# Attention beside Strassen-Winograd products: two visits of eight key tiles for every head, and QKV sums kept in DRAM

## The chip, the cores and the metric

One core of one Trainium2 chip runs the kernel in a single launch. The time is device microseconds of one execution. TensorE (PE) does the matrix products and loads its weights beside them (PEld), VectorE (DVE), ScalarE (ACT) and GpSimd (POOL) do the elementwise work, and SyncE (SP) issues the DMA transfers. PSUM holds the products' results in eight banks of 128 x 512 float32 values.

## What is computed

```python
def _A_ref(x, wqkv, wo):             # x 1 x 2048 x 1024, wqkv 1024 x 3072, wo 1024 x 1024
    H = 32; Dh = 32
    qkv = (x @ wqkv).reshape(B, S, 3, H, Dh).transpose(2, 0, 3, 1, 4)
    q, k, v = qkv[0], qkv[1], qkv[2]
    p = softmax(einsum("bhqd,bhkd->bhqk", q, k) * Dh ** -0.5)
    o = einsum("bhqk,bhkd->bhqd", p, v)
    return o.transpose(0, 2, 1, 3).reshape(B, S, D) @ wo
def _B_ref(x, dft_seq_re, dft_seq_im, dft_hid_re, dft_hid_im):
    a = einsum("bsd,ed->bse", x, dft_hid_re)
    b = einsum("bsd,ed->bse", x, dft_hid_im)
    return einsum("ts,bse->bte", dft_seq_re, a) - einsum("ts,bse->bte", dft_seq_im, b)
out = concatenate([_A_ref(...), _B_ref(...)], axis=-1)
```

## The kernel before

There are two kinds of work for TensorE. The dense parts are QKV (`qkv`), the product over the hidden dimension (`dense1`), the product over the sequence (`dense2`) and the output projection (`project`). Each is one level of a Winograd form with seven products instead of eight, numbered p = 1 to 7. Each float32 operand is split into a high and a low part of a faster format (`halves`: a cast and a subtraction), and three matmuls (high-high, low-high, high-low) make one product. A group of 12 or 24 such matmuls fills one PSUM bank, which is then evicted. The list `fills` holds these matmuls in their order; 6720 of them run.

The other kind is attention over 32 heads, in three streams. S (`scores`) makes the scores of a block of queries with 1024 keys in two matmuls (line 1322); VectorE takes the row maxima (line 1328) and ScalarE the exponentials and their sums (line 1331). T (`transposed`) makes the transposed scores, 16 key tiles of 128 keys by four query blocks of 512 (line 1447), and ScalarE turns each of these 64 products into a tile of exponentials (line 1456). V, the visits, multiplies the exponentials of some key tiles with V in column strips of 32 (line 1479) into one bank, and VectorE adds the bank to the head's output (lines 1499 and 1501). A visit starts only when the exponentials of its tiles are there, save the last one.

Rings limit what runs ahead. The exponentials have 23 tiles in heads 0 to 7 (5 `ptl`, 18 `pt`), and a head has visits of 5, 5 and 6 key tiles (`ENDS`). From head 8 on (`H2`) eight more tiles (`ptm`, pool `pt2`) come from memory that the QKV stage held as slots 12 to 15, and a head has two visits of eight (`ENDS2`). S and T have two PSUM buffers each, and the banks `pd` of fills and visits two.

QKV runs in twelve steps (`STEPS`). Steps 0 to 4 take the first three pairs of Q/K blocks (`PAIRS`) and V before attention starts. Steps 5 to 9 take the other five pairs in the order p = 1, 2, 6, 5, 3, and steps 10 and 11 take p = 7 and p = 4 for all pairs and V. A late pair's running sum X lies in a slot of SBUF (16 to 19, and 15 + b - `PAIRS` in general). For p = 7 two kept sums are loaded from DRAM through a ring of four `c` tiles (`CR`, function `kept`), and for the Q/K groups the third of them stays in its `c` tile until p = 4 of the same group, which follows at once: the groups of p = 7 and p = 4 alternate. In `dense1`, sums of rows 0 to 3 lie in slots 16 to 19 and those of rows 4 to 7 go by DRAM (`Far`, arrays `x_d`).

The order of all instructions is written out when the kernel is built, by a planner (`Plan`) that imitates the engines with fixed costs. For TensorE it picks among the heads of the streams and the next fill: a visit first, then T, then S, and a fill if none of these can start, or if the fills lag behind `nf / (FILL - RES) <= done / ATT`. Some constants steer it: `LEAD` and `SST` hold S back when it is too far ahead of T, `STOCK` (us) and `PATIENCE` put a visit off until enough work is queued on ScalarE, and `MARGIN` adds time to the landing of a DMA before VectorE's work on it is placed. The other engines, and SyncE's queue of DMAs, get the order that the imitated run gave; each engine then runs its list in order.

Of the kernel before, what the change touches and what calls it, by code (L numbers as in the profile page):

```python
# [16 lines left out]
P = 128  # L17
S = 2048
D = 1024
H = 32  # L20
# [4 lines left out]
NPT, NPT2 = 23, 8  # L25
H2 = 8
# [4 lines left out]
NLOW = 5  # L31
ENDS, ENDS2 = (0, 5, 10, 16), (0, 8, 16)
# [193 lines left out]
def kernel(  # L226
# [32 lines left out]
    u_d = [[dram.tile([P, NB], F32, name=f"u_d{g}_{k}") for k in (2, 3, 4)] for g in range(24)]  # L259
# [3 lines left out]
    x_d = [[{w: dram.tile([P, NB], F32, name=f"x_d{i}_{m}_{w}") for w in (1, 6, 5)} for m in range(2)] for i in range(4)]  # L263
# [8 lines left out]
    def slot(i, shape, dt=F32R):  # L272
        if i < 12:
            return big.tile(shape, dt, name=f"slot{i}", tag=f"slot{i}")
        if i < 16 and "pt2" in late:
            return op_pool().tile(shape, dt, name=f"slot{i}", tag=f"slot{i}")
        if i < 20:
            att()
            return late["sums" if i > 15 else "low"].tile(shape, dt, name=f"slot{i}", tag=f"slot{i}")
# [70 lines left out]
    def more():  # L350

        if "pt2" not in late:
            late["low"].release()
            late["pt2"] = tc.alloc_tile_pool(name="pt2", bufs=1, reuse_waits="tile")
        return late["pt2"]

# [7 lines left out]
    SUMS = (16, 17, 18, 19)  # L364
# [13 lines left out]
    SST = 12  # L378
    LEAD = 4
    PATIENCE = 2  # L380
    STOCK = 2.4
# [4 lines left out]
    ATT = H * (128 * MM + 16 * PV) + (3 * H2 + 2 * (H - H2)) * SWITCH  # L386
# [64 lines left out]
    slots = [[] for _ in range(40)]  # L451
# [169 lines left out]
    def qkv():  # L621
        VR, SG = Ring(NV), Ring(2)
        sq, tx, t1x = ([[] for _ in range(8)] for _ in range(3))
        sv, u_st = [[] for _ in range(4)], [[[], [], []] for _ in range(24)]
# [28 lines left out]
        def load_x(x, k):  # L653
            where[0] = ahead if x < 5 else within
            p = STEPS[x][0]
            if x < 5:
                i = 8 * ((x + 1) % 2) + k
                i = i if i < 12 else 20 + i
            else:
                i = (8 * (x - 5) + k) % 12 if x < 11 else (16, 8)[k // 4] + k  # L660
            XS[x, k] = moving(i, x_terms(p, k, x >= 5), (tx_d[k], tx[k]) if x == 3 else (t1x_d[k], t1x[k]) if x == 2 else None)

        def load_v_weight(x, c):
            where[0] = ahead if x < 5 else within
            p = STEPS[x][0]
            WV[x, c] = moving((28 if x in (1, 3) else 12 if x == 10 else 0 if x == 11 else 36) + c, w_terms(p, lambda i, j: wv[i, 4 * j + c], sv_d[c], sv[c]), (sv_d[c], sv[c]) if p == 6 else None)
# [83 lines left out]
        def gather(p, g, result, early, scale=None):  # L750
# [3 lines left out]
            whole_u3 = g < 16  # L754
# [11 lines left out]

            if p == 7:
                U4, U2 = kept(2), kept(0)
            elif p == 4:
                U3 = u3.pop(g) if whole_u3 else kept(1)  # L770

            def finish(ps, last):
                if p == 5 and early:
                    box = {}
                    old, users = ER.take()

                    def product(e="DVE"):
# [12 lines left out]
                    att_gate.extend([c, e, u_st[g][0][-1]])  # L790
                    return e
                if p == 1:
# [45 lines left out]
        def qk_group(x, W, b, n):  # L838
# [52 lines left out]
        for x, (p, blocks, v) in enumerate(STEPS[:10]):  # L891
# [35 lines left out]
            if x == 4:  # L927
                for u in ahead[0].users + slots[28:]:
# [6 lines left out]
        for x in (10, 11):  # L935
            for t in range(8):
                v_group(x, t)
                if x == 11 and t < 4:
                    load_x(11, 4 + t)
                elif x == 10 and t < 2:  # L940
                    for k in range(2):
                        load_x(10, 4 + 2 * t + k)
                elif x == 10 and 2 <= t < 6:
                    load_x(11, t - 2)
                    load_v_weight(11, t - 2)
# [115 lines left out]
    def dense1():  # L1061
# [26 lines left out]
        def load_b(x, n):  # L1088
            p = ORDER[x]
            B[x][n] = moving((8 * x + n) % 12, b_terms(p, n), (t1_d[n], t1[n]) if p == 6 else None)  # L1090
# [5 lines left out]
        for x, p in enumerate(ORDER):  # L1096
            for i in range(8):
# [4 lines left out]
                if p == 1:  # L1102
                    X[i] = accs(SUMS[i]) if i < 4 else [Far(x_d[i - 4][m]) for m in range(2)]
# [13 lines left out]
    def load_ab(step, k):  # L1117
# [11 lines left out]
        AB[step, k] = moving((8 * (7 + step) + k) % 12, terms, (t2_d[m][k], t2[m][k]) if p == 6 else None)  # L1129
# [47 lines left out]
    def op_pool():  # L1177
        if "op" not in late:
            att().release()
            qk0.release()  # L1180
            late["pt2"].release()
# [5 lines left out]
    def behind():  # L1187

        over.extend(o for h in o_st for o in h)
        for i in (*range(12, 16), *range(20, 28)):  # L1190
# [6 lines left out]
    def project():  # L1197
# [60 lines left out]
        for x, p in enumerate(ORDER):  # L1258
            for i in range(8):
                j, t = divmod(i, 4)  # L1260
                if p == 1 and i % 2 == 0:
                    X[i // 2] = accs(16 + i // 2)
                if p == 7 and i % 2 == 0:
                    Y[i // 2] = accs(12 + i // 2)
# [33 lines left out]
    def scores(h):  # L1298
# [12 lines left out]
        for n, (qt, c) in enumerate([(k % 4, k // 4) for k in range(8)] + [divmod(k, 2) for k in range(8, 32)]):  # L1311
# [30 lines left out]
            if n == 5 and h:  # L1342
                sums(h - 1)
# [87 lines left out]

    def transposed(h):
        moved = mine[h][4]
        todo, ends_with = [], []
        po = {}
        oold, ouse = ot_r.take()
        ends = ENDS if h < H2 else ENDS2
        for t in range(NS):
            for j in range(4):
# [9 lines left out]
                def ex(box=box, here=here):  # L1449
                    if here < NLOW:  # L1450
                        box["t"] = att_low().tile([P, NB], F32, name="ptl", bufs=NLOW)
                    elif here < NPT:
                        box["t"] = att().tile([P, NB], F32, name="pt", bufs=NPT - NLOW)
                    else:
                        box["t"] = more().tile([P, NB], F32, name="ptm", bufs=NPT2)
# [3 lines left out]
                def more_exp(a=a, ex=ex, here=here, users=users, box=box, t=t, j=j):  # L1459
# [3 lines left out]
                    return t, j, box, e, pt_r.users[here], a  # L1463
# [3 lines left out]
                if t + 1 in ends and j >= 4 - PEND:  # L1467
# [3 lines left out]
            if t + 1 in ends:  # L1471
                load, vuse = vts[h]
                t0 = ends[ends.index(t + 1) - 1]

                def pv(k, part, t=t, t0=t0):
                    if k == t0:
                        po["p"] = psD.tile([P, NB], F32, name="pd")
                    for _, j, box, *_ in part:
                        nc.tensor.matmul(  # L1479
                            po["p"][j * DH : j * DH + DH, :], VT[h][:, k, :], box["t"], start=(k == t0), stop=(k == t),  # L1480
                            tile_position=(0, j * DH),
                        )

                visit = []
                for k in range(t0, t + 1):
                    if k == t:
                        todo += [m() for m, _ in ends_with]
                    part = [x for x in todo if x[0] == k]
                    visit.append(op("PE", PV + (SWITCH if k == t0 else 0), lambda k=k, part=part, pv=pv: pv(k, part),
                                    [*load[: t // 4 + 1], *(x[3] for x in (todo if k == t0 else part)), *(x[1] for x in (ends_with if k == t0 else ()))],  # L1490
                                    [vuse, *(x[4] for x in part)]))
                ends_with = []
                v = visit[-1]
                todo = []

                def gather_o(t0=t0):
                    if t0 == 0:
                        po["o"] = att_low().tile([P, NB], F32, name="ot", bufs=2)
                        nc.vector.tensor_copy(po["o"], po["p"])
                    else:  # L1500
                        nc.vector.tensor_tensor(out=po["o"], in0=po["o"], in1=po["p"], op=ALU.add)

                e = op("DVE", EVAC, gather_o, [v] + (oold if t0 == 0 else []), [ouse], -1)
                streams["V"].append((visit[0], h, e, visit[1:]))
            if t % 4 == 3 and h + 2 < H:
                load_qk_op(h + 2, 1, t // 4, [Tops[h][-1], Sops[h][-1]])
        if h + 2 < H:
# [3 lines left out]
            load_v(h + 2)  # L1511
        return e, po, ouse
# [19 lines left out]
    for h in range(H):  # L1532
        if h == H2:
            pt_r.n %= NPT
            pt_r.users.extend(sum((slots[i] for i in range(12, 16)), []) for _ in range(NPT2))
        if h + 1 < H:
            scores(h + 1)
        else:
            sums(h)
        result(h, *transposed(h))  # L1540
# [15 lines left out]
    while nf < len(fills) or any(place[n] < len(s) for n, s in streams.items()):  # L1556
# [19 lines left out]
        pl.MARGIN["DVE"] = 3 if heads and t_on[0] else 2  # L1576
# [52 lines left out]
        if ok:  # L1629
# [5 lines left out]
            if n == "V":  # L1635
                banks.append(heads[n][2])
# [43 lines left out]
```

## Time and profile before

| what | value |
|---|---|
| median of 3 runs | 2942.34 us (2941.63 to 2942.66) |
| the profiled execution | 2942.34 us, span of its instructions 2940.6 us |
| granted TensorE clock | 1.000 |
| matmuls on TensorE | 14922 |
| DMA | 585 MB on SyncE's queue, share 61.8% |

In the rows of the profile, a group reads: line, engine, operation, output<-input by the program's names, count, then busy time in us, the mean of one in ns, and the idle time just before them with what ended it. `psS` and `psT` are the banks of the streams S and T, `pd` that of fills and visits, `qs`, `ks` and `qx` are Q and K, `c` a loaded sum, `e` an evicted result. A window's row gives for each engine the busy time and the number of instructions in the stretch.

### The profile page before, as it was taken

The numbers are of one execution on the slowest core, as the hardware profiler recorded it, in microseconds if no ns is written. First come the engines' busy times: TensorE is split into PE (matmuls) and PEld (weight loads), VectorE is DVE, ScalarE is ACT, GpSimd is POOL, SyncE is SP. The second block draws the span as 40 slices with busy tenths as digits, with TensorE's granted clock in tenths as the row PEclk, the third lists the DMA queues.
The fourth block names the chain that finished last, engine by engine and source line by source line (L and its number), as shares of the span: only waits on it lengthen the run. The fifth ranks groups of instructions, "written<-read, shape, count | busy, mean of one in ns | idle before, by whom it ended". The sixth has DMA issues, their size and how long they took to land.

```text
span 2940.6 us, 45778 instructions
## 1 busy us (share of the span) xinstructions
PE 2931.5 (100%) x14922; PEld 2151.9 (73%) x14922; DVE 2275.1 (77%) x3103; ACT 2271.7 (77%) x4322; POOL 956.6 (33%) x746
## 2 busy tenths in 40 slices
PE   9999999999999999999999999999999999999999
PEld 7887777677777777777777777777777777677787
DVE  6778888788877877877677888787787788886685
ACT  5348888888888888888888888888888888886331
POOL 2323435222204432231112454433112454454142
PEclk9999999999999999999999999999999999999999
DMA  9975658666637655675434776655434786665753
GB/s 348 356 249 183 200 183 276 227 213 225 218 103 229 217 176 164 212 226 166 158 101 147 239 231 205 189 180 169 129 113 132 216 270 200 194 182 191 264 194 126
DMA packets 393880, 587.96 MB, mean 200 GB/s; under 512 B 112782, under 2 KB 114574, under 8 KB 393518
## 3 DMA queue, kind: packets, MB, share of 16 engines
q1 hardware_dynamic: 393644, 585.05, 61.8%
q8 instruction: 120, 1.97, 0.3%
q14 instruction: 116, 0.95, 0.1%
HBM read 421.30 MB, written 163.59 MB: 199 GB/s over the span
## 4 chain that ended last, share of the span: by engine, by line
PE 98%; DVE 1%; DMA 1%; ACT 0%; SPq 0%; issue 0%; DVEq 0%; ACTq 0%
PE pd L421 44%; PE psT L1447 16%; PE psS L1322 16%; PE pd L1479 15%; PE psT L421 6%; DVE negm L1328 0%; DMA er<-in_xa 0%; DVE l L531 0%; DMA qs<-qk_d 0%; PE psT L443 0%; ACT psS L1331 0%; DVE h L528 0%; PE pd L443 0%; ACT slot L527 0%; DVE slot L531 0%
## 5 line engine op out<-in xcount | busy, mean ns | idle before, releaser
L1328 DVE TENSOR_REDUCE negm<-psS 128x1 f32<-128x1024 f32 x1024 | 1242.8, 1221 | 226.4 <-PE psS L1322 215.2
L1331 ACT ACTIVATE psS<-psS,negm 128x1024 f32<-128x1024 f32 x1024 | 1223.9, 1195 | 71.8 <-DVE negm L1328 70.0
L421 PE MATMUL pd<-slot,h 128*128 128x512 f32 x3360 | 1144.0, 390 | 0.0
L1456 ACT ACTIVATE pt<-psT 128x512 f32<-128x512 f32 x1296 | 782.6, 697 | 260.1 <-PE psT L1447 237.2
L1447 PE MATMUL psT<-qs,ks 128*128 128x512 f32 x2048 | 794.3, 394 | 1.3 <-DMA qs<-qk_d 1.3
L421 PEld LDWEIGHTS pd<-slot,h 128*128 128x128 f32 x3360 | 630.7, 188 | 132.0
L421 PE MATMUL pd<-slot,l 128*128 128x512 f32 x1680 | 654.6, 390 | 0.0
L507 POOL TENSOR_TENSOR raw<-raw,g 128x512 f32<-128x512 f32 x295 | 382.6, 1304 | 483.8 <-DVE l L531 63.8
L1447 PEld LDWEIGHTS psT<-qs,ks 128*128 128x128 f32 x2048 | 381.8, 188 | 137.3 <-issue 45.3
L1322 PE MATMUL psS<-ks,qs 128*128 128x512 f32 x1552 | 473.4, 390 | 1.2 <-ACT psS L1331 1.2
L531 POOL TENSOR_TENSOR l<-raw,h 128x512 fp32r<-128x512 f32 x157 | 202.5, 1290 | 554.6 <-PE psT L1447 236.6
L531 POOL TENSOR_TENSOR slot<-raw,slot 128x512 fp32r<-128x512 f32 x156 | 201.0, 1293 | 518.0 <-DVE slot L528 146.3
L421 PEld LDWEIGHTS pd<-slot,l 128*128 128x128 f32 x1680 | 315.3, 188 | 67.0 <-issue 0.8
L1479 PE MATMUL pd<-pt,vt 128*32 128x512 f32 x2592 | 345.8, 594 | 0.0
L1322 PEld LDWEIGHTS psS<-ks,qs 128*128 128x128 f32 x1552 | 290.8, 188 | 64.0 <-ACT psS L1331 3.8
L1331 ACT ACTIVATION_READ_ACCUMULATOR psS<-psS,negm 128x1 f32 x1024 | 321.6, 314 | 0.0
L1456 ACT ACTIVATE ptm<-psT 128x512 f32<-128x512 f32 x392 | 242.6, 715 | 49.7 <-PE psT L1447 46.7
L1456 ACT ACTIVATE ptl<-psT 128x512 f32<-128x512 f32 x360 | 223.5, 708 | 31.0 <-PE psT L1447 30.2
L1479 PEld LDWEIGHTS pd<-pt,vt 128*32 128x32 f32 x2592 | 89.4, 110 | 180.3 <-issue 168.2
L421 PE MATMUL pd<-slot,slot 128*128 128x512 f32 x768 | 193.0, 391 | 0.0
L421 PEld LDWEIGHTS pd<-slot,slot 128*128 128x128 f32 x768 | 144.1, 188 | 31.2
L528 DVE CAST h<-raw 128x512 fp32r<-128x512 f32 x321 | 149.1, 467 | 14.5 <-PE pd L421 12.3
(139 smaller groups left out, 2323.8 us busy)
## 6 DMA issues: line engine op xcount, KB each, us to landing
raw<-in_ct SPq DMA_DIRECT2D x224, 256.0 KB
g<-in_ct SPq DMA_DIRECT2D x128, 256.0 KB
c<-u_d SPq DMA_DIRECT2D x120, 256.0 KB
qk_d<-e SPq DMA_DIRECT2D x52, 512.0 KB
qs<-qk_d SPq DMA_DIRECT2D x128, 192.0 KB
ks<-qk_d SPq DMA_DIRECT2D x128, 192.0 KB
raw<-ab_d SPq DMA_DIRECT2D x96, 256.0 KB
g<-ab_d SPq DMA_DIRECT2D x80, 256.0 KB
```

The source lines that it names most:

```text
L421: nc.tensor.matmul(box["ps"], a[1]((a[0].hi, a[0].lo)[u]()), b[1]((b[0].hi, b[0].lo)[v]()), start=k == 0, stop=k == n - 1)
L507: return (nc.gpsimd if e == "POOL" else nc.vector).tensor_tensor(out=dest(), in0=dest() if a is None else a.get(), in1=other["q"] if "q" i ...
L528: return nc.vector.tensor_copy(hi(), raw())
L531: return (nc.gpsimd if e == "POOL" else nc.vector).tensor_tensor(out=lo(), in0=raw(), in1=f(hi()), op=ALU.subtract)
L1322: nc.tensor.matmul(p[:, i * NB : i * NB + NB], (QX[0] if own else QS[h % 2])[:, qt * P : qt * P + P], KS[h % 2][:, c * 1024 + i * NB : c * ...
L1328: nc.vector.tensor_reduce(out=ST["negm"][:, c, qt : qt + 1], in_=box["p"], axis=AX.X, op=ALU.max, negate=True)
L1331: nc.scalar.activation(box["p"], box["p"], AF.Exp, bias=ST["negm"][:, c, qt : qt + 1], accum_out=ST["sums"][:, c, qt : qt + 1])
L1447: nc.tensor.matmul(box["p"], KS[h % 2][:, t * P : t * P + P], QS[h % 2][:, j * NB : j * NB + NB], start=True, stop=True)
L1456: nc.scalar.activation(box["t"], box["p"], AF.Exp)
L1479: nc.tensor.matmul(po["p"][j * DH : j * DH + DH, :], VT[h][:, k, :], box["t"], start=(k == t0), stop=(k == t), tile_position=(0, j * DH),)
```

## The change

Every head gets visits of eight key tiles: `H2` is 0, and a list `CUTS` of cumulated key tiles over all heads takes the place of `ENDS`. The ring of exponentials has 31 tiles from the first head on, 13 of them in the pool `atl`; the pool `pt2` is gone. To free the memory, slots 16 to 19 are given up in the QKV stage and in `dense1`: the sums of the late pairs are stored in DRAM after p = 1, 6 and 5 and loaded again for p = 2, 6, 5 and 3, and `dense1` treats rows 0 to 3 as it did rows 4 to 7. The third sum of a Q/K group is stored at p = 7 and loaded at p = 4. All groups of p = 7 now come before those of p = 4, first V then Q/K at p = 7, first Q/K then V at p = 4, with the x pieces of p = 4 loaded among the Q/K groups of p = 7. Slots are renumbered. The small work of a head's sums (`sums`) is created in `transposed` rather than in `scores`. The planner's constants `SST`, `LEAD`, `STOCK` and `MARGIN` change.

```diff
-NPT, NPT2 = 23, 8
-H2 = 8
+NPT, NPT2 = 31, 8
+H2 = 0
-NLOW = 5
-ENDS, ENDS2 = (0, 5, 10, 16), (0, 8, 16)
+NLOW = 13
+BLOCKS, BLOCKS2 = (8, 8), (8,)
+CUTS = []
+for k in range(H2):
+    CUTS += [16 * k + sum(BLOCKS[: i + 1]) for i in range(len(BLOCKS))]
+while not CUTS or CUTS[-1] < 16 * H:
+    CUTS.append(min(16 * H, (CUTS[-1] if CUTS else 0) + BLOCKS2[len(CUTS) % len(BLOCKS2)]))
...
-    SUMS = (16, 17, 18, 19)
+    SUMS = (12, 13, 14, 15)
...
-    SST = 12
-    LEAD = 4
+    SST = 14
+    LEAD = 1
     PATIENCE = 2
-    STOCK = 2.4
+    STOCK = 1.4
...
-    ATT = H * (128 * MM + 16 * PV) + (3 * H2 + 2 * (H - H2)) * SWITCH
+    ATT = H * (128 * MM + 16 * PV) + len(CUTS) * SWITCH
...
-                i = (8 * (x - 5) + k) % 12 if x < 11 else (16, 8)[k // 4] + k
+                i = (8 * (x - 5) + k) % 12 if x < 11 else (12, -4)[k // 4] + k
...
-            whole_u3 = g < 16
+            whole_u3 = False
...
+            stored = p in (2, 3, 5, 6) and A is None
             if p == 7:
                 U4, U2 = kept(2), kept(0)
+            elif stored:
+                U = kept({2: 3, 6: 3, 5: 0, 3: 2}[p])
...
+                if A is None and p in (1, 5, 6):
+                    box = {}
+                    old, users = ER.take()
+                    i = {1: 3, 6: 0, 5: 2}[p]
+                    def keep():
+                        box["y"] = pre.tile([P, NB], F32, name="e", tag="e", bufs=NE)
+                        if p > 1:
+                            combine(box["y"], U[0](), ps(), ALU.add, scale)
+                        elif scale is None:
+                            nc.vector.tensor_copy(box["y"], ps())
...
+                    e = evac_op(keep, last, ER, [users, *(U[1] if p > 1 else [])], [*old, *([U[2]] if p > 1 else [])])
+                    u_st[g][i].append(op("SP", ISSUE, lambda: nc.sync.dma_start(u_d[g][i], box["y"]), [e], [users], rank, 256))
+                    return e
+                if stored:
+                    return result(ps, last, U[0], U[1], [U[2]], ALU.add)
...
-                    X[2 * b], X[2 * b + 1] = accs(15 + b - PAIRS)
+                    X[2 * b] = X[2 * b + 1] = None
...
-        for x in (10, 11):
-            for t in range(8):
+        for x, p in ((10, 7), (11, 4)):
+            for t in range(8 if x == 10 else 0):
                 v_group(x, t)
...
-        for b in range(8):
-            W = [piece(w_terms(p, lambda i, j: wqk[b + 8 * i][:, 4 * j : 4 * j + 4, :], None, None)) for p in (7, 4)]
-            for n in range(2):
-                qk_group(10, W[0], b, n)
-                qk_group(11, W[1], b, n)
+            for b in range(8):
+                W = piece(w_terms(p, lambda i, j: wqk[b + 8 * i][:, 4 * j : 4 * j + 4, :], None, None))
+                for n in range(2):
+                    qk_group(x, W, b, n)
+                if x == 10:
+                    load_x(11, (b + 4) % 8)
+            if x == 10:
+                for c in range(4):
+                    load_v_weight(11, c)
+        for t in range(8):
+            v_group(11, (t + 4) % 8)
...
-                    X[i] = accs(SUMS[i]) if i < 4 else [Far(x_d[i - 4][m]) for m in range(2)]
+                    X[i] = accs(SUMS[i]) if i < 0 else [Far(x_d[i][m]) for m in range(2)]
...
-                if t + 1 in ends and j >= 4 - PEND:
+                if 16 * h + t + 1 in CUTS and j >= 4 - PEND:
                     ends_with.append((more_exp, a))
...
-        pl.MARGIN["DVE"] = 3 if heads and t_on[0] else 2
+        pl.MARGIN["DVE"] = 2.5 if heads and t_on[0] else 1
```

More of the change, by code (lines that the diff above doesn't have):

```diff
@@ L274, in slot @@
             return big.tile(shape, dt, name=f"slot{i}", tag=f"slot{i}")
-        if i < 16 and "pt2" in late:
+        if i < 16:
+            att()
+            return late["low"].tile(shape, dt, name=f"slot{i}", tag=f"slot{i}")
+        if i >= 40:
             return op_pool().tile(shape, dt, name=f"slot{i}", tag=f"slot{i}")
-        if i < 20:
-            att()
-            return late["sums" if i > 15 else "low"].tile(shape, dt, name=f"slot{i}", tag=f"slot{i}")
         if i < 28:
@@ L1430, in load_v @@
         vts[h] = (made, users)
+    PO = {}
+    todo, ends_with = [], []
     def transposed(h):
         moved = mine[h][4]
[L1434 removed]
         po = {}
[L1436 to L1437 removed]
+        PO[h] = (po, *ot_r.take())
+        if not todo:
+            sums(h)
         for t in range(NS):
@@ L1470, in transposed @@
                     todo.append(more_exp())
[L1471 to L1504, printed above, removed]
@@ L1532 @@
     for h in range(H):
-        if h == H2:
-            pt_r.n %= NPT
-            pt_r.users.extend(sum((slots[i] for i in range(12, 16)), []) for _ in range(NPT2))
         if h + 1 < H:
             scores(h + 1)
-        else:
-            sums(h)
-        result(h, *transposed(h))
+        transposed(h)
     dense1()
```

97 lines of the change are left out of this document (65 added, 32 removed).

## The prediction

> **What bounds the kernel now.** I read the page first: engines, slices, the chain of work that ended last.
>
> ```profile
> span 2940.6 us, 45778 instructions
> PE 2931.5 (100%) x14922; PEld 2151.9 (73%) x14922; DVE 2275.1 (77%) x3103; ACT 2271.7 (77%) x4322; POOL 956.6 (33%) x746
> ...
> PE 98%; DVE 1%; DMA 1%; ACT 0%; SPq 0%; issue 0%; DVEq 0%; ACTq 0%
> ```
>
> TensorE is busy for the whole span and is 98% of the chain. The span of 2940.6 us lies in a profiled execution of 2942.34 us, which is also the median of the runs shown, so a change of the span goes straight onto 2942.34. Next, everything that TensorE waited for (the waits of that engine: total us, times, longest):
>
> ```profile
> PE pd L1555 <- DVE qs L303: 1.5, 1, 1.5
> PE psT L443 <- DVE acc L799: 1.3, 1, 1.3
> PE psT L1447 <- DMA qs<-qk_d: 1.3, 1, 1.3
> PE psS L1322 <- ACT psS L1331: 1.2, 3, 0.5
> ```
>
> That is 5.3 us, 2.8 of it at the start, which the change does not touch. 2.5 us are left. So time can fall only by less TensorE work, and idle time that the change creates is paid in full. The chain in order of time gives the prices of that work (start, us, what; x counts instructions):
>
> ```profile
> 27.35 5.44 PE psT L421 x24
> ...
> 270.63 4.43 PE pd L1479 x40
> ...
> 908.77 7.00 PE pd L1479 x64
> ```
>
> An ordinary product is 5.44/24 = 0.227 us. A visit to the products with V costs 4.43 us for five key tiles and 7.00 for eight. What the other engines do while this goes on stands in the windows (stretch, length, then busy time and count of PE, PEld, DVE, ACT, POOL, clock, DMA share, GB/s):
>
> ```profile
> 245.00:877.00 632.00, 630.74 (x3263) 448.82 (x3261) 508.48 (x700) 537.73 (x1032) 202.15 (x158) 1.00 0.64 209
> 1033.00:1191.00 158.00, 158.00 (x826) 114.36 (x825) 120.05 (x161) 135.17 (x260) 45.86 (x36) 1.00 0.59 182
> 2748.00:2784.00 36.00, 36.00 (x160) 29.78 (x160) 28.46 (x44) 8.10 (x13) 5.52 (x4) 1.00 0.90 321
> ```
>
> The first stretch holds heads 0 to 7 with 24 visits, the second two later heads with four visits. ScalarE idles 94.3 us in the first (11.8 per head) and 22.8 in the second (11.4 per head, 5.7 per visit of 7.0): during a visit it has only what was queued before. Outside visits it is nearly full, so ScalarE sets how fast attention advances, and the matmuls of the dense parts ("fills") take the rest of TensorE. The third stretch follows attention: 160 products of the second dense stage were left over, and they cover the way from the last head's output to the projection.
>
> **The change, part by part.** *Visits.* Heads 0 to 7 go from 5+5+6 key tiles to 8+8. The price of a tile is the slope between the quoted visits, (7.00 - 4.43)/3 = 0.857 us, so a visit costs about 0.15 us beside its tiles (7.00 - 8 x 0.857 = 0.14, 4.43 - 5 x 0.857 = 0.15). Eight visits disappear: 8 x 0.15 = 1.2 us less TensorE work. All other matmuls keep number and shape. Seen from ScalarE, heads 0 to 7 go from 11.8 to about 11.4 us idle per head, so attention ends some 3 us earlier; that is no time by itself, only 3 us more of leftover fills.
>
> *31 tiles from head 0.* From head 8 on the kernel before already has 31, visits of eight and no stall of TensorE; heads 0 to 7 become such heads. The exponentials cost the same. I add nothing.
>
> *QKV sums by DRAM.* The evictions do not change in number, only where they read and write:
>
> ```profile
> L681 DVE TENSOR_TENSOR slot<-slot,pd 128x512 f32<-128x512 f32 x12 | 8.2, 682 | 3.1 <-PE pd L421 2.9
> L681 DVE TENSOR_TENSOR e<-c,pd 128x512 f32<-128x512 f32 x16 | 10.9, 680 | 0.2 <-POOL e L531 0.2
> ```
>
> With the sum in a kept slot the addition takes 682 ns, from a loaded `c` into an `e` tile 680 ns: VectorE's work is unchanged. The DMAs are not. For each of the ten late Q/K sums a store at p = 1 and loads at p = 2, 6, 5 and 3 come in; for all 16 Q/K sums a store at p = 7 and a load at p = 4: 82 transfers. In the first dense stage rows 0 to 3 go as rows 4 to 7 went: three stores and five loads for each of eight sums, 64 transfers. The rows of DMA (queue: packets, MB, share; then issues, and one issue from SyncE's timeline):
>
> ```profile
> q1 hardware_dynamic: 393644, 585.05, 61.8%
> ...
> c<-x_d SPq DMA_DIRECT2D x40, 256.0 KB
> ...
> x_d<-e SPq DMA_DIRECT2D x24, 256.0 KB
> ...
> 2774.66 0.32 SPq L971 DMA_DIRECT2D c<-u_d  x1
> ```
>
> 146 transfers of 256 KB are 38 MB on 585, or 6.5%: share 62 to 66%. In the dense stage this is shown harmless: the 40 loads and 24 stores of rows 4 to 7 ran beside attention, and none stands among TensorE's waits; I take 0. SyncE issues 146 more instructions at 0.32 us, 47 us of its 2940; queued behind them are loads of K, Q and V, which the planner ranks first (-2), so I take 0 here too.
>
> *Order of p = 7 and p = 4.* This is the place where I find a cost. Before, the Q/K groups of p = 7 and p = 4 alternate; after, all 16 of p = 7 come first, and between them the eight x pieces of p = 4 are loaded. The stretch that holds these groups before, and its transfers:
>
> ```profile
> 634.00:787.00 153.00, 153.00 (x794) 107.90 (x793) 126.97 (x178) 128.65 (x246) 42.25 (x34) 1.00 0.70 235
> ...
> qk_d<-e SPq DMA_DIRECT2D x24, 512.0 KB
> qk_d<-e SPq DMA_DIRECT2D x24, 256.0 KB
> ...
> ks<-qk_d SPq DMA_DIRECT2D x8, 192.0 KB
> qs<-qk_d SPq DMA_DIRECT2D x8, 192.0 KB
> ```
>
> 24 groups in 153 us: 6.4 us each, 235 GB/s at share 0.70, that is 336 GB/s at a full share. A p = 7 group of the changed kernel moves 512 + 256 KB of results, two `c` loads (512), its `u3` store (256), half of a weight piece of two loads (256) and half of an x piece of two loads (256): 2048 KB = 2.1 MB in 6.4 us, 328 GB/s. Attention's own are 16 x 192 KB for K and Q in the 153 us, and from the code about 1.9 MB more (x, V, sums, output): 5 MB, 33 GB/s. Together 361 GB/s over 16 x 6.4 = 102 us, or 37 MB. One earlier stretch ran as hot:
>
> ```profile
> 17.00:74.00 57.00, 57.00 (x253) 47.16 (x252) 39.50 (x61) 26.74 (x47) 9.20 (x8) 1.00 1.02 366
> ```
>
> 366 GB/s with TensorE never idle. So the bounds: at 366/1.02 = 359 GB/s the 37 MB take 103 us, 1 us too long; at 336 they take 110 us, 8 us too long. ScalarE holds attention back and cannot give TensorE other work, so the excess is idle TensorE. VectorE, at 127 of 153 us, also gets about 1.5 us per group more (the third sum, the subtraction and split of the x piece), part of which GpSimd, at 42 of 153, can take. I take 2 us, near the row that ran at that rate, because the p = 4 groups that follow move less (one `c` load, no `u3` store, no x piece) and take up some lag; the range keeps 0 to 8.
>
> The Trainium skill, "DMA: Bandwidth & Descriptors", Specifications, gives about 358 GB/s as one core's limit to memory. By that rule the 37 MB take 103.3 us and the sum has +1 where the row of 336 GB/s would give it +8; the row of 366 GB/s lies slightly above the page's figure.
>
> *Planner constants.* LEAD 4 to 1 with SST 12 to 14 limits how far scores run ahead of the transposed products:
>
> ```profile
> L1447 PE MATMUL psT<-qs,ks 128*128 128x512 f32 x2048 | 794.3, 394 | 1.3 <-DMA qs<-qk_d 1.3
> L1322 PE MATMUL psS<-ks,qs 128*128 128x512 f32 x1552 | 473.4, 390 | 1.2 <-ACT psS L1331 1.2
> ...
> L1322 PE MATMUL psS<-ks,qx 128*128 128x512 f32 x496 | 149.1, 392 | 0.0
> ```
>
> Both have 2048 matmuls and a score takes two, so scores go at 0.5 per product. The new limit is (1 + t/4) x 33/14 scores after t products of a head: 2.4 at its start, rising by 0.59 per product; it can bite only early in a head. STOCK 2.4 to 1.4 lets a visit start with 1 us less queued on ScalarE. VectorE's allowance for landing falls from 3 to 2.5 us, and outside attention from 2 to 1. What is queued behind a late landing on VectorE is the next row maximum, and ScalarE waits for that. I cost these at 0, between -3 us of attention (it could also be better ordered) and +1.0 us for each of 64 visits; the cover is the leftover of fills.
>
> **Sum.** -1.2 (visits) + 2 (p = 7 groups) + 0 = about +0.8 us: 2942.34 + 0.8 = 2943.1 us, no change that a measurement of this kernel could tell (0.2%, 5.9 us, is about what it can).
>
> **The rivals.** *Slower, attention falls behind.* If each visit leaves ScalarE idle longer by d, attention ends 64 d later, and fewer fills remain for the way to the projection. The 36 us after attention hold some unneeded cover. Its last pieces before the first group of the projection:
>
> ```profile
> 2774.16 1.30 POOL L531 TENSOR_TENSOR slot<-raw,slot 128x512 fp32r<-128x512 f32 x1 [3.76 <-DVE slot L531]
> 2777.47 0.68 DVE L531 TENSOR_TENSOR slot<-raw,slot 128x512 fp32r<-128x512 f32 x1
> ...
> 2787.27 0.69 DVE L984 COPY slot<-psT 128x512 f32<-128x512 f32 x1 [0.16 <-PE psT L421]
> ```
>
> The first group's sum is copied at 2787.3, its 12 products began 2.7 us earlier, at 2784.4; its operands were there by 2778.2. Spare: 6 us, plus the 3 us of earlier attention. From d = 0.15 us (64 x 0.15 = 9.6) TensorE idles; at d = 0.4 it is 25.6 - 9 = 17 us, 2959 us; at the full 1.0 us 55 us, 2997 us. For it: STOCK is lowered by just 1.0. Against it: a visit is also put off while a score or transposed product can start, and that rule stays, so the queue is mostly full at 2.4 or more anyway.
>
> *Slower, DMA-bound p = 7 groups.* The upper bound above and its lag on VectorE: +8 us on TensorE, and K and Q loads late by as much. From 7 us on it decides: 2942.3 - 1.2 + 8 to 14 = 2949 to 2955. For it: 361 of 336 GB/s. Against it: 366 GB/s was borne once. The Trainium skill, "TensorE: Matmul & The Clock Gate", The HAM clock gate, halves the clock after an idle window of about 3.4 us. The trace shows the clock at 1.00 in every stretch quoted and no wait over 1.5 us, so no run here shows it; by that rule a single stall of that length would cost, as an estimate from the page's window, half of 3.4 us or 1.7 us on top.
>
> *Faster.* All 2.5 us of waits inside attention go, and no new one comes: 2942.3 - 1.2 - 2.5 = 2938.6, or 0.13%: still within 0.2%. Over 5.9 us would need the start's waits as well (1.2 + 5.3 = 6.5). That the larger ring for heads 0 to 7 does nothing for the time is the forecast itself: it serves ScalarE, which is not the bound.
>
> **How the numbers follow.** Forecast, within 0.2%: 0.60. Attention behind by enough: 0.17. DMA-bound groups beyond the limit: 0.20. Faster by over 0.2%: 0.03. The range starts at 2938 (the faster case) and reaches to 2957, which takes in the DMA case and the smaller half of the attention case; the likeliest case alone spans 2938 to 2948.
>
> **What would show it.** Right: 64 visits of 7.00 us, TensorE's waits 3 to 8 us in all, a DMA share near 0.9 or more and some new waits of TensorE or VectorE on `c`, `raw` or `qs` where p = 7 runs, around 540 to 660 us; after attention about 150 to 175 products before the projection. Wrong: ScalarE's idle per head in the later heads above 12.5 us and a gap of TensorE after the last visit (attention behind), or a stretch of many microseconds idle at p = 7 (DMA), or waits on `x_d` in the first dense stage, which I costed at nothing.

## The result, and the profile after

The changed kernel takes 2951.61 us (median of 7 runs, 2947.95 to 2953.59), the kernel before 2942.35 us beside it: a ratio of 1.003, with a 95% interval of 1.0018 to 1.0042. That is 9.3 us slower, over the 0.2% bound of the prediction (the interval begins just under it). It lies inside the stated range, but not in the likeliest case, no change. The prediction had two slower cases, with chances of 0.17 and 0.20, but each stood for a mechanism that, as shown below, did not make the time. That the range held is therefore luck. The profiled execution took 2953.59 us.

The page of the changed kernel: span, busy time, the DMA queue, the chain by engine.

```profile
span 2951.8 us, 45994 instructions
PE 2936.2 (99%) x14922; PEld 2152.3 (73%) x14922; DVE 2277.5 (77%) x3104; ACT 2279.4 (77%) x4322; POOL 945.2 (32%) x737
...
q1 hardware_dynamic: 414668, 623.33, 64.4%
...
PE 93%; DMA 3%; DVE 2%; ACT 0%; issue 0%; SPq 0%; POOL 0%; DVEq 0%; POOLq 0%; ACTq 0%
```

TensorE has the same 14922 matmuls. The 38 MB of added transfers are there (585 to 623 MB). What is new is in the chain: TensorE falls from 98% to 93%, and DMA and VectorE take 5%. TensorE's own waits in the changed kernel:

```profile
PE psS L1343 <- ACT psS L1352: 6.5, 7, 2.7
PE psT L419 <- ACT slot L525: 1.5, 1, 1.5
PE pd L1585 <- DVE qs L308: 1.5, 1, 1.5
PE psT L1469 <- DMA qs<-m_d: 0.9, 2, 0.5
PE psT L419 <- DVE slot L529: 0.2, 1, 0.2
```

The wait of a score matmul for its PSUM bank has gone from 1.2 to 6.5 us in these two executions, and a wait at the projection (L419 on a slot) is new.

This list leaves out small delays, slow-clock products and waits of weight loads. So I also added up, from the traces, by how much the starts of consecutive matmuls lie further apart than the usual 0.227 us (0.318 ahead of a visit; the fixed steps around a visit left out). I call this TensorE's lost time. The stages are cut by the count of fills. Each row is one profiled execution (us), with the median time of the label's runs beside it; the labels are explained with the experiments. The two must be read with care: executions of one kernel lie up to 9 us apart, and the profiled one is the slowest for changed, margin_back and alt_rows and the fastest for rows_sbuf, visits_back and rotate. A difference of two or three microseconds in one column is therefore no proof.

| kernel | median | ratio to before (95%) | start | QKV, late pairs | dense1 | dense2 | projection | lost in all | span less lost |
|---|---|---|---|---|---|---|---|---|---|
| before | 2942.3 | | 4.3 | 1.7 | 0.0 | 2.8 | 0.0 | 8.7 | 2931.9 |
| changed | 2951.6 | 1.0030 (1.0018 to 1.0042) | 4.0 | 2.6 | 5.8 | 7.0 | 2.6 | 22.1 | 2929.7 |
| before_null | 2949.0 | 1.0022 (1.0013 to 1.0031) | 4.2 | 4.1 | 0.0 | 6.8 | 0.0 | 15.1 | 2932.1 |
| before_null2 | 2944.5 | 1.0010 (1.0001 to 1.0019) | 4.3 | 1.0 | 1.8 | 3.5 | 0.0 | 10.6 | 2932.1 |
| before_consts | 2948.4 | 1.0021 (1.0012 to 1.0030) | 3.9 | 0.2 | 1.8 | 3.9 | 2.1 | 11.8 | 2932.5 |
| after_null | 2955.0 | 1.0044 (1.0032 to 1.0057) | 4.5 | 8.6 | 0.5 | 3.6 | 4.9 | 22.2 | 2928.6 |
| margin_back | 2962.5 | 1.0067 (1.0054 to 1.0079) | 4.0 | 9.4 | 6.7 | 5.5 | 6.5 | 32.1 | 2929.3 |
| pace_back | 2963.1 | 1.0076 (1.0063 to 1.0088) | 3.8 | 11.9 | 1.0 | 7.6 | 5.5 | 29.8 | 2929.3 |
| rows_sbuf | 2951.5 | 1.0031 (1.0019 to 1.0043) | 4.1 | 1.2 | 1.5 | 7.5 | 3.4 | 17.7 | 2928.9 |
| alternate | 2947.9 | 1.0025 (1.0016 to 1.0034) | 3.6 | 5.0 | 0.1 | 3.1 | 5.1 | 16.9 | 2929.2 |
| alt_rows | 2951.0 | 1.0028 (1.0018 to 1.0039) | 3.7 | 5.0 | 0.6 | 6.9 | 6.8 | 23.0 | 2930.2 |
| visits_back | 2950.7 | 1.0027 (1.0017 to 1.0038) | 3.7 | 6.2 | 0.0 | 2.6 | 2.5 | 15.1 | 2931.2 |
| rotate | 2950.5 | 1.0031 (1.0019 to 1.0042) | 3.5 | 2.7 | 4.4 | 3.7 | 2.0 | 16.3 | 2929.7 |
| rotate_rows | 2947.3 | 1.0023 (1.0014 to 1.0032) | 3.2 | 4.7 | 2.5 | 4.8 | 2.3 | 17.4 | 2928.7 |

Read from the first two rows: the work of TensorE (span less lost) fell by 2.2 us, its lost time rose by 13.4 us, and the span rose by 11.2 us (the medians differ by 9.3 us). The whole question is where lost time comes from.

The largest single piece shows one mechanism. This is the chain of work of the changed kernel in order of time, around 1008 us (start, us, what; the matmuls left out):

```profile
987.90 6.07 DMA raw<-in_wd
...
993.98 6.37 DMA g<-in_xb
...
1000.48 1.14 POOL raw L505
...
1003.18 1.29 POOL raw L505
...
1004.50 1.50 DVE slot L526
1006.00 1.14 DVE negm L1349
...
1007.22 1.21 ACT psS L1352 x2
```

Two loads of the first dense stage take over 6 us each, GpSimd's subtractions wait for them, VectorE has a cast of that operand at the head of its list and stands until 1004.5, and the row maximum of the scores comes only behind it. ScalarE then frees the score bank at 1008.4, and TensorE, whose next instruction is a matmul into that bank, has stood since 1005.8. No engine was busy all the time from 1000 to 1008 us: GpSimd 6.41 of 8 us, the others less, DMA share 0.75. The delay passed from the transfers through the lists of four engines, each of which runs in order. That the order had been written for an earlier landing is how I read it; the planner's expected time is not in the trace. The added transfers have a part here: from 970 to 1012 us SyncE issued 11 transfers of `x_d`, for 3 in the kernel before, and one wait of GpSimd, 4.3 us, is put down to `x_d<-e`.

### The profile page after: what moved, and what is told of

Read it like the earlier page. It is cut to its first block, busy times and chain, and to the rows that moved or that the text cites. A ratio compares the mean times of both kernels' runs of the same rounds, so it can differ in the third digit from the quotient of the medians.

```text
span 2951.8 us, 45994 instructions
## 1 busy us (share of the span) xinstructions
PE 2936.2 (99%) x14922; PEld 2152.3 (73%) x14922; DVE 2277.5 (77%) x3104; ACT 2279.4 (77%) x4322; POOL 945.2 (32%) x737
## 4 chain that ended last, share of the span: by engine, by line
PE 93%; DMA 3%; DVE 2%; ACT 0%; issue 0%; SPq 0%; POOL 0%; DVEq 0%; POOLq 0%; ACTq 0%
PE pd L419 42%; PE psT L1469 15%; PE psS L1343 15%; PE pd L1506 14%; PE psT L419 6%; DVE negm L1349 1%; DMA c<-u_d 1%; DMA qs<-m_d 0%; ACT psS L1352 0%; DMA er<-in_xa 0%; DMA raw<-in_ct 0%; POOL raw L505 0%; DVE h L526 0%; DVE l L529 0%; DMA g<-in_xb 0%
## 5 line engine op out<-in xcount | busy, mean ns | idle before, releaser
L419 PE MATMUL pd<-slot,h 128*128 128x512 f32 x3376 | 1153.7, 390 | 0.1
L1476 ACT ACTIVATE pt<-psT 128x512 f32<-128x512 f32 x1188 | 721.0, 703 | 196.0 <-PE psT L1469 184.2
L419 PEld LDWEIGHTS pd<-slot,h 128*128 128x128 f32 x3376 | 634.2, 188 | 135.5 <-issue 2.5
L419 PE MATMUL pd<-slot,l 128*128 128x512 f32 x1688 | 658.2, 390 | 0.0
L1476 ACT ACTIVATE ptl<-psT 128x512 f32<-128x512 f32 x860 | 521.3, 699 | 156.1 <-PE psT L1469 142.6
L505 POOL TENSOR_TENSOR raw<-raw,g 128x512 f32<-128x512 f32 x275 | 357.7, 1307 | 437.4 <-DMA raw<-ab_d 73.7
L529 POOL TENSOR_TENSOR l<-raw,h 128x512 fp32r<-128x512 f32 x173 | 223.1, 1290 | 723.4 <-PE psT L1469 254.2
L419 PEld LDWEIGHTS pd<-slot,l 128*128 128x128 f32 x1688 | 317.2, 188 | 66.9 <-issue 0.8
L529 POOL TENSOR_TENSOR slot<-raw,slot 128x512 fp32r<-128x512 f32 x167 | 215.3, 1292 | 433.3 <-DVE slot L526 215.0
L1506 PE MATMUL pd<-pt,vt 128*32 128x512 f32 x2376 | 315.0, 594 | 0.0
L1506 PE MATMUL pd<-ptl,vt 128*32 128x512 f32 x1720 | 243.8, 594 | 0.2
L1506 PEld LDWEIGHTS pd<-pt,vt 128*32 128x32 f32 x2376 | 83.2, 110 | 168.9 <-issue 159.5
L419 PE MATMUL pd<-slot,slot 128*128 128x512 f32 x768 | 193.5, 390 | 0.0
L419 PEld LDWEIGHTS pd<-slot,slot 128*128 128x128 f32 x768 | 144.2, 188 | 30.4
```

What stands on the lines that cost most here:

```text
L419: nc.tensor.matmul(box["ps"], a[1]((a[0].hi, a[0].lo)[u]()), b[1]((b[0].hi, b[0].lo)[v]()), start=k == 0, stop=k == n - 1)
L505: return (nc.gpsimd if e == "POOL" else nc.vector).tensor_tensor(out=dest(), in0=dest() if a is None else a.get(), in1=other["q"] if "q" i ...
L529: return (nc.gpsimd if e == "POOL" else nc.vector).tensor_tensor(out=lo(), in0=raw(), in1=f(hi()), op=ALU.subtract)
L1476: nc.scalar.activation(box["t"], box["p"], AF.Exp)
L1506: nc.tensor.matmul(PO[g][0]["p"][j * DH : j * DH + DH, :], VT[g][:, r, :], box["t"], start=first, stop=stop, tile_position=(0, j * DH),)
```

## The experiments

I began with three theories. *Allowance*: VectorE is placed too close to the expected landing (`MARGIN`). *Transfers*: the added transfers make landings late. *Pace*: `SST`, `LEAD` and `STOCK` hold attention back.

**margin_back**

```diff
-        pl.MARGIN["DVE"] = 2.5 if heads and t_on[0] else 1
+        pl.MARGIN["DVE"] = 3 if heads and t_on[0] else 2
```

> The changed kernel with VectorE's allowance for landing alone set back (3 us in attention, 2 outside). Theory 'allowance' (VectorE is placed too close to the expected landing of a DMA, stands at its head when the DMA is late, and the row maximum queued behind it makes ScalarE and then TensorE wait): most of the 12 us of new idle TensorE goes, 2943 to 2946 us, and TensorE's waits on psS fall from 6.5 us to under 3. Theory 'transfers' (the 146 added DMA transfers make landings late whatever the allowance): 2948 to 2951 us. Theory 'pace' (SST, LEAD, STOCK): no change, 2949 to 2952 us.

Measured: 2962.5 us, 11 us slower than the changed kernel. The theory of the allowance falls as I had put it: with more allowance there were more waits. The waits on `psS` rose:

```profile
PE psS L1343 <- ACT psS L1352: 8.8, 9, 2.3
PE psT L419 <- ACT slot L525: 3.2, 1, 3.2
```

**pace_back**

```diff
-    SST = 14
-    LEAD = 1
+    SST = 12
+    LEAD = 4
...
-    STOCK = 1.4
+    STOCK = 2.4
```

> The changed kernel with SST 12, LEAD 4 and STOCK 2.4 set back, and nothing else. Theory 'pace': attention ends earlier, over 150 products of the dense stages are left after the last visit (110 in the changed kernel), 2943 to 2946 us. Theories 'allowance' and 'transfers': 2948 to 2952 us, with the waits on psS still 4 us or more.

Measured: 2963.1 us, 11 us slower, with 83 products left after attention for 110. The theory of pace falls too, with the opposite sign: in the one order tried of each, the old constants were worse than the new ones in this structure. The two times lie some 8 us above the slowest of the eight other kernels of the changed structure.

**rows_sbuf**

```diff
-                    X[i] = accs(SUMS[i]) if i < 0 else [Far(x_d[i][m]) for m in range(2)]
+                    X[i] = accs(SUMS[i]) if i < 4 else [Far(x_d[i][m]) for m in range(2)]
```

> The changed kernel with rows 0 to 3 of the first dense stage kept in slots 12 to 15 again, which are free by then: 64 transfers fewer. Theory 'transfers': the 5.8 us that TensorE idles between 800 and 1500 us go, 2945 to 2947 us. Theory 'allowance': the same stretch gains 0 to 2 us, 2949 to 2952 us.

Measured: 2951.5 us, no change of the time. Lost time in `dense1` is 1.5 us for 5.8, as the theory of transfers had it, but it is 0.5 us in after_null, which has all 64 transfers; so this is no proof that they caused it.

**alternate** (cut to the order of the groups)

```diff
-            whole_u3 = False
+            whole_u3 = g < 16
...
+        for t in range(8):
+            v_group(10, t)
...
+        for b in range(8):
+            W = [piece(...) for p in (7, 4)]
+            for n in (1, 0):
+                qk_group(10, W[0], b, n)
+                qk_group(11, W[1], b, n)
+        for c in range(4):
+            load_v_weight(11, c)
+        for t in range(8):
+            v_group(11, (t + 4) % 8)
```

> The changed kernel with the Q/K groups of p = 7 and p = 4 alternating again and their third sum kept in its c tile: 32 transfers fewer, and the densest stretch of DMA spread out. Theory 'transfers' in the form of the prediction (p = 7 groups bound by DMA): the 2.4 us of idle TensorE between 480 and 800 us go, 2948 to 2950 us, and up to 8 us if the lag is carried on, 2943 us. Theory 'allowance': within 2 us of 2951 us.

Measured: 2947.9 us, a ratio of 1.0025 (1.0016 to 1.0034), whose interval overlaps that of the changed kernel. The time is about what the theory of transfers said, but the trace does not show the gain where it was expected: lost time in the late QKV steps is 5.0 us for 2.6, most of it in one wait of a visit for an eviction:

```profile
PE pd L1507 <- DVE e L681: 2.9, 1, 2.9
```

After these four, none of the parts tried owned the lost time: taking one away moved it to other places. So a fourth theory. *Chosen order*: the planner's order is rebuilt by any edit, each order meets late landings at a few places by chance, and the order of the kernel before happens to meet hardly any. It is tested by edits that mean nothing.

**before_null**

```diff
-    MAX, EVAC, CAST, BIT = 1.22, 0.685, 0.415, 0.275
+    MAX, EVAC, CAST, BIT = 1.22, 0.69, 0.415, 0.275
```

> The kernel before with the planner's cost of an eviction 0.69 us for 0.685, an edit of no meaning that makes the planner write another order. Theory 'chosen order' (the order of the kernel before happens to meet hardly a late landing, and any other order of the same work pays 5 to 20 us in waits of TensorE): 2947 to 2962 us. Theory 'transfers' (the waits come from what the change adds): 2941 to 2944 us.

Measured: 2949.0 us, ratio 1.0022 (1.0013 to 1.0031). Five nanoseconds in an imitated cost, with the same matmuls, visits and megabytes moved, cost 6.7 us. The planner wrote another order and moved some small work from VectorE to GpSimd (769 instructions of GpSimd for 746). TensorE's waits are of the kinds of the changed kernel:

```profile
PE psS L1322 <- ACT psS L1331: 4.1, 8, 1.0
PE psT L443 <- DVE acc L799: 1.5, 1, 1.5
PE pd L1555 <- DVE qs L303: 1.5, 1, 1.5
PE pd L1479 <- DVE c L683: 1.1, 1, 1.1
```

A late landing is not behind all of them. The two longest waits for the score bank, before 1642 and 2438 us, have no transfer in the chain that leads to them. What VectorE and GpSimd did before the first (start, us):

```profile
1636.88 1.44 DVE L528 CAST h<-raw 128x512 fp32r<-128x512 f32 x1
1638.36 1.67 DVE L531 TENSOR_TENSOR l<-raw,h 128x512 fp32r<-128x512 f32 x1
1639.95 2.34 DVE L1328 TENSOR_REDUCE negm<-psS 128x1 f32<-128x1024 f32 x2
...
1636.74 5.78 POOL L507 TENSOR_TENSOR raw<-raw,g 128x512 f32<-128x512 f32 x4 [1.50 <-DMA raw<-ab_d]
```

VectorE's cast took 1.44 us and its subtraction 1.67 us while GpSimd worked beside them. Of the 475 casts of this trace with no work of GpSimd beside them none took more than 0.43 us, and no such subtraction took more than 0.70 us. The row maximum stood behind these two, ScalarE behind it, and TensorE behind ScalarE. The wait before 1848 us in the changed kernel, 1.2 us long, came in the same way: a cast of 1.53 us and a subtraction of 1.67 us. (GpSimd's own work began when a load landed, so a landing may still have set which work fell together.) So an order can lose in at least two ways: by a landing that comes late for it, and by small work of VectorE that falls beside GpSimd's.

**before_null2**

```diff
-    ISSUE = 0.46
+    ISSUE = 0.465
```

> The kernel before with the planner's cost of a DMA issue 0.465 us for 0.46. Theory 'chosen order': 2946 to 2955 us, as the first edit without meaning gave 2949.0 us. Rival (that one was an accident): 2941 to 2944 us.

Measured: 2944.5 us, ratio 1.0010 (1.0001 to 1.0019). Slower again, by 3.2 us: a little under the band that the theory gave, and just over the rival's. The price of another order of the kernel before is thus 3 and 7 us in two draws. Both were slower, which fits an order better than most, but two draws do not prove that it is one.

**before_consts**

```diff
-    SST = 12
-    LEAD = 4
+    SST = 14
+    LEAD = 1
...
-    STOCK = 2.4
+    STOCK = 1.4
...
-        pl.MARGIN["DVE"] = 3 if heads and t_on[0] else 2
+        pl.MARGIN["DVE"] = 2.5 if heads and t_on[0] else 1
```

> The kernel before with the four planner constants of the changed kernel (SST 14, LEAD 1, STOCK 1.4, VectorE's allowance 2.5 and 1), nothing else. Theory 'chosen order': 2947 to 2962 us, waits scattered over all stages. Theory 'constants suit the change' (they are worth 11 us each there and are bad here): 2950 us or more, with fewer products left after attention. Theory 'transfers': 2941 to 2945 us.

Measured: 2948.4 us, within what the edits without meaning gave. The new constants are not bad for the structure before beyond that.

**after_null**

```diff
-    MAX, EVAC, CAST, BIT = 1.22, 0.685, 0.415, 0.275
+    MAX, EVAC, CAST, BIT = 1.22, 0.69, 0.415, 0.275
```

> The changed kernel with the planner's cost of an eviction 0.69 us for 0.685. Theory 'chosen order': the changed kernel's order is one of many, 2946 to 2960 us, with waits at other places. Rival (the new constants and places give a wait at fixed points): 2950 to 2953 us with the 2.8 us wait near 1008 us again.

Measured: 2955.0 us, 3.4 us over the changed kernel, with intervals of the ratio that overlap. The wait of 2.7 us near 1008 us is gone, and new ones stand at the late QKV steps (8.6 us for 2.6). The piece of the chain quoted above thus belongs to one order and does not come with the change as such. (In rotate, whose order is the same up to the projection, it is there again.)

**visits_back**

```diff
-H2 = 0
+H2 = 8
...
-BLOCKS, BLOCKS2 = (8, 8), (8,)
+BLOCKS, BLOCKS2 = (5, 5, 6), (8,)
```

> The changed kernel with visits of 5, 5 and 6 key tiles for heads 0 to 7 again (72 visits), the rest as changed. The price of a visit, from the intervals around one in the trace (0.09 us before it, 0.11 behind the last product, 0.11 two products later), is 0.3 us, or 2.5 us for eight: the span without TensorE's waits goes from 2929.7 to 2932 us. By the prediction's 0.15 us it would be 2930.9 us. The time is 2952 to 2956 us if the waits stay, within 2946 to 2962 us if theory 'chosen order' holds.

Measured: 2950.7 us; the span without lost time is 2931.2 us, between the two forecasts, against 2928.6 to 2930.2 in the nine kernels with 64 visits and 2931.9 to 2932.5 in the four of the kernel before. Averaged over the five with 72 and the nine with 64 visits it is 2932.0 and 2929.3 us, a difference of 2.7 us. The direct pair, visits_back and changed, differs by 1.5 us, about as much as the nine kernels differ among themselves. So the fewer visits do give something, 1.5 to 2.7 us, and the gain is lost in the waits; between the two forecasts this run does not decide.

**alt_rows** (the edits of alternate and rows_sbuf together)

> The changed kernel with both edits that take transfers away: Q/K groups of p = 7 and p = 4 alternate, and rows 0 to 3 of the first dense stage stay in slots 12 to 15 (96 transfers fewer). Theory 'transfers': the gains add, 2943 to 2946 us, and TensorE's waits between 480 and 1500 us are under 2 us. Theory 'chosen order': anything from 2944 to 2960 us, not ordered by the number of transfers.

Measured: 2951.0 us. The gains do not add, and the time isn't ordered by the number of transfers: 96 transfers fewer give the time of the changed kernel. As the main cause the theory of transfers falls; 50 added transfers remain in this kernel too.

One column of the table is not scattered. At the projection the changed kernel and all its variants lose 2.0 to 6.8 us; before and both edits without meaning to it lose none (before_consts 2.1). The chain of the changed kernel there:

```profile
2787.43 1.37 PE psT L419 x6
2788.81 0.02 issue
2788.83 0.64 ACT slot L525
...
2789.49 0.42 DVE slot L529
2789.92 5.08 DMA raw<-o_d
...
2795.56 1.14 ACT slot L525 x2
2796.70 0.02 issue
2796.73 0.70 DVE slot L529
```

The split of a projection piece follows right on products of the second dense stage (L419), its buffer then lets the next load of `o_d` go, and TensorE stands around 2795. The diff turns the slots of the dense stages by 8 (`(8 * x + n + 8) % 12`), so that the last step lies in slots 0 to 7 rather than 4 to 11, while the projection still puts its first pieces of wo into slots 0 to 3.

**rotate**

```diff
-            1: ([20, 24], 0), 7: ([4, 8], 20), 2: ([0, 4], 24), 6: ([8, 0], 20),
-            5: ([4, 8], 24), 3: ([0, 4], 20), 4: ([8, 0], 24),
+            1: ([20, 24], 8), 7: ([0, 4], 20), 2: ([8, 0], 24), 6: ([4, 8], 20),
+            5: ([0, 4], 24), 3: ([8, 0], 20), 4: ([4, 8], 24),
```

> The changed kernel with the projection's slots 0, 4 and 8 turned to 8, 0 and 4, nothing else; TensorE's order is the same up to the projection's first groups. Theory 'slots' (the change turns the dense stages' slots by 8, so that the last step of the second dense stage lies in slots 0 to 7, and the projection's first four pieces of wo, in slots 0 to 3, can be split only behind it): TensorE's wait at the first projection groups, 2.6 us in the changed kernel's trace, goes, 2948 to 2949 us. Rival 'cover' (attention ends later, 110 products are left after it for 160, too few to hide the way from the last head to the projection): the wait stays, 2951 to 2952 us.

Measured: 2950.5 us, between the two forecasts. TensorE's wait on ScalarE's slot is gone from its list, with 110 products left as before, so the rival (too little cover between attention and the projection) falls for that wait. visits_back says the same: 162 products were left and it waited all the same. But a wait some groups later took its place:

```profile
PE psS L1343 <- ACT psS L1352: 5.0, 7, 2.1
PE pd L1585 <- DVE qs L308: 1.5, 1, 1.5
PE psT L419 <- POOL slot L529: 1.3, 1, 1.3
```

Lost time at the projection is 2.0 us for 2.6. The first place is explained; little time came back.

For the wait that took its place the rival stands. before_consts, with the slots of the kernel before and 102 products left after attention, waits in the same way, at 2811 us where rotate waits at 2812 us:

```profile
PE psT L421 <- POOL slot L531: 1.8, 1, 1.8
```

The kernel before and its two edits without meaning, with 160, 138 and 183 products left, have no such wait. That few leftover products make it is argued from these six kernels (rotate_rows, with 110, has it too), not tested by an edit.

**rotate_rows** (the same on rows_sbuf)

> The same turn of slots on the kernel with rows 0 to 3 of the first dense stage in slots 12 to 15. By 'slots' its wait of 3.4 us at the projection goes: 2948 us for 2951.5; by 'cover' it stays.

Measured: 2947.3 us, ratio 1.0023 (1.0014 to 1.0032), for 1.0031 (1.0019 to 1.0043) of rows_sbuf: the better value as forecast, with intervals that overlap. It is the fastest kernel of the changed structure that ran, and still slower than the kernel before. In all, the four orders of the structure before took 2942.3 to 2949.0 us, and the ten kernels of the changed structure 2947.3 to 2963.1 us.

## Why the prediction was right or wrong

*What bounds the kernel*: right. TensorE stayed the bound, and idle time was paid in full.

*Visits*: the sign was right, the size probably too small. I took 0.15 us for a visit beside its tiles, from the lengths of visits. The steps just outside a visit belong to it too; with them it is about 0.3 us, by which eight visits give some 2.5 us for my 1.2. The spans without lost time give 1.5 to 2.7 us.

*p = 7 groups*: the rate was near, the sum behind it was not. The window with these 16 groups in the changed kernel (columns as in the prediction):

```profile
531.00:626.00 95.00, 94.68 (x479) 68.97 (x478) 82.77 (x115) 83.39 (x162) 25.66 (x21) 1.00 0.90 308
```

The DMA share is 0.90, as said, at 308 GB/s for my 361, and TensorE was busy for 94.68 of 95 us. I had put the eight x pieces of p = 4 between these groups; the trace loads seven of them before 520 us, ahead of the window, so 29 MB moved in it for my 37. Over the late QKV steps lost time rose by 0.9 us for my 2, but that column goes from 0.2 to 11.9 us over the kernels, so the agreement shows little. The rival of the DMA-bound groups is out.

*Attention behind*: out in the form that I gave it, though one sign appeared. In the heads from 1041 to 1198 us ScalarE idles 22.4 us, or 11.2 per head, as before:

```profile
1041.00:1198.00 157.00, 157.00 (x825) 113.64 (x821) 117.79 (x157) 134.57 (x258) 47.14 (x37) 1.00 0.64 205
```

Attention ended 20 us later and left 110 products for 160. As shown, the first wait at the projection did not hang on that; the one that stood behind it may, and it is 1 to 2 us. STOCK and LEAD, which I held against the change, were better for it by 11 us, in the one order tried. The times of 2959 and 2997 us that I gave this case leave out my own 1.2 us of visits.

*The step that failed* is the 0 for the planner's constants and for all that is only moved. I gave single waits a price, from what each part of the change does, and took the 2.5 us of waits inside attention before as a level that stays. It does not stay: edits without meaning lift the lost time from 8.7 to 10.6 and 15.1 us. By the table, `dense2`, whose work the change does not touch, went from 2.8 to 7.0 us, and to 6.8 us in before_null. My sum therefore started from an order better than the others that ran, and every part of the change gives that order up. The slots turned by 8, which I mentioned in one sentence as renumbered and did not price, made a wait within the 2.6 us lost at the projection, of which turning them back returned 0.6 us.

*How much of the 9.3 us is which?* An edit without meaning costs the kernel before 3 to 7 us, the change saves some 1.5 to 2.7 us of visits, and the rest is more lost time in the new structure. As an estimate from two orders each, with the same two eviction costs: before 2942.3 and 2949.0, changed 2951.6 and 2955.0, so the means differ by 7.6 us, while the two members of a pair differ by 6.7 and 3.4. What in the structure makes its orders worse stays open. Fewer transfers (rows_sbuf, alternate, alt_rows) gave 2948 to 2952 us and did not settle it, and the new place of `sums` and the renumbered slots of QKV were not tried alone.

## What to carry to other kernels

When an engine is 99% busy and the order of all lists is written out ahead, a change of 0.1 to 0.3% can't be read from one build: first change something without meaning and see how far the time moves. Price the loss of the present order as a cost of any edit, and look what small work falls beside that of another engine. When buffers are renumbered, follow the numbers to the next stage that uses them.

## What the runs showed of the hardware

The wait near 1008 us cost more than its length. The timeline of TensorE in the changed kernel around it:

```profile
1005.43 0.39 PE L419 MATMUL pd<-slot,h 128*128 128x512 f32 x1
1008.48 1.19 PE L1343 MATMUL psS<-ks,qs 128*128 128x512 f32 x2 [2.66 <-ACT psS L1352]
1009.47 0.63 PE L419 MATMUL pd<-slot,h 128*128 128x512 f32 x1
1009.89 0.63 PE L1469 MATMUL psT<-qs,ks 128*128 128x512 f32 x1
...
1012.24 0.40 PE L419 MATMUL pd<-slot,h 128*128 128x512 f32 x1
```

And a window over what follows the wait:

```profile
1008.60:1012.20 3.60, 3.60 (x9) 2.88 (x10) 2.30 (x3) 3.28 (x7) 0.50 (x1) 0.53 0.95 333
```

After 2.66 us of idle, products start 0.42 us apart for some 3 us at a granted clock of 0.53, and take 0.63 us for 0.39. The wait of 2.8 us beyond the usual step became 4.5 us of lost time. The Trainium skill, "TensorE: Matmul & The Clock Gate", The HAM clock gate, puts such a drop behind an idle window of about 3.4 us; here a shorter idle time was enough, and the measurement decides. The extra 1.7 us are what I had estimated for such a stall.

The length of one idle time does not decide alone. In pace_back one of the same length left the clock at 1.00, and in margin_back a shorter one, of 2.04 us, was followed by 0.54 (first the matmuls with their idle time, then the windows behind them; pace_back, then margin_back):

```profile
563.12 1.48 PE L1506 MATMUL pd<-ptl,vt 128*32 128x512 f32 x10 [2.66 <-DVE e L681]
563.20:566.60 3.40, 3.40 (x35) 1.01 (x39) 1.62 (x3) 1.09 (x2) 0.00 (x0) 1.00 1.05 357
...
1302.66 0.76 PE L1343 MATMUL psS<-ks,qs 128*128 128x512 f32 x2 [2.04 <-ACT psS L1352]
1303.00:1306.70 3.70, 3.70 (x11) 2.78 (x10) 1.60 (x2) 3.70 (x8) 0.67 (x1) 0.54 1.03 370
```

What does decide is not shown here.
